# Block-sparse attention and a rational feed-forward layer on one core: GpSimd leaves the decoding of weights and the splitting of keys and queries to the vector and the activation engine

## Chip, cores, metric

One core of one Trainium2 chip. The metric is the time on the device, in microseconds, of one execution of the program; lower is better. Engines are named as in the profile: PE (matrix products), PEld (its weight loads), DVE (the vector engine), ACT (the activation engine), POOL (GpSimd), SP (the engine that issues all DMAs here).

## What is computed

Attention of 4 batches, 8 heads, 768 positions and 64 dimensions, masked by blocks of 32, then a feed-forward layer whose activation is a rational function:

```python
scores = scale * np.matmul(q, k.transpose(0, 1, 3, 2))
mask = np.abs(blk_i - blk_j) <= 1
mask = mask | (blk_i == 0) | (blk_j == 0) | (blk_i == n_blocks - 1) | (blk_j == n_blocks - 1)
# and for each block of queries three sampled blocks of keys
attn = softmax(np.where(mask, scores, -1e9))
x = np.matmul(attn, v)                      # as 3072 tokens of 512
h = x @ w_in                                # 512 x 2048
P = a[0] + a[1] * h + a[2] * h**2 + a[3] * h**3
Q = 1.0 + np.abs(b[0]) * np.abs(h) + np.abs(b[1]) * h**2
out = (P / (Q + 1e-06)) @ w_out             # 2048 x 512
```

`w_in` and `w_out` come as 64-bit numbers, so the kernel decodes them to 32 bits itself.

## The kernel before

**Weights.** `weights()` loads 32 pieces of 128 x 512 numbers (16 of `w_in`, 16 of `w_out`) as pairs of 32-bit words into two buffers `wl`. `convert` (one input) makes a 32-bit float of the upper word; `pack1`, `pack2`, `pack3` (L447, L450, L453, all DVE) put the lost bits in. A piece of `w_out` lies in `dw` then, and is split into a high part `wo_h` (`out_high`, one input) and a low part `wo_l = dw - wo_h` (`out_low`, L464, two inputs). A piece of `w_in` is decoded in place in `wi`; when four are there, ACT has taken their largest value and DVE has made a scale of it (`scw`), `three` scales each (`scaled`, `dw<-wi,scw`), takes a 16-bit high part (`high`, `wi<-dw`) and subtracts it (`low`, L511, two inputs).

**Keys and queries.** They are scaled and split in the same way into 16-bit high and low parts, 128 x 512 a tile: keys in `rest()` (tile `hl`), queries in `prep_q()` (tile `hlq` out of `ldq`, of which there is one buffer). The high part is a one-input instruction, the low part (L391) is DVE's. PE then transposes them.

**Attention and units.** `attention()` works on one block of 32 queries of all heads: scores (`sp`, L913), their maxima on DVE (L923), exponentials on ACT (`pr`, L941), transposes (`pt`, `pT`), products with values (`av`, L1039). ACT copies sampled key blocks for batch 0 (`kx`, L866). The feed-forward runs in 96 units of 256 tokens by 256 columns: PE's products into `ph` (L1150 to L1152), ACT's `sq`, `tt`, `ab`, `rr`, seven DVE instructions, the last of which are L1185 (`gh`), L1188, L1191 and L1195 (`gl`), and PE's products with `wo_h` and `wo_l` (L1206 to L1208).

**What sets the order.** Nothing is scheduled by hand: each piece of work is an `Op` with an engine, a price in nanoseconds, what it comes after, buffers it takes and a priority. `issue()` goes through them like a simulation and writes the program in the order in which they come up, each engine's queue in order. An `Op` whose engine is a dictionary may go to any engine in it; the first one is preferred. `among` makes that dictionary, but only for keys that stand in `ALT = "copsk"`; for any other key it gives the home engine alone:

```python
ALT = "copsk"

def among(key, home, **prices):
    d = {{"ve": VE, "sc": SC, "po": PO}[n]: p for n, p in prices.items()}
    return {home: d[home], **(d if key in ALT else {})}
```

`times` is the helper that does all one-input work, so its instructions have its lines: L150 on ACT, L154 on POOL and DVE (L152 for a plain copy). While POOL works, `issue` delays a DVE piece that reads no PSUM by half of what is left of POOL's (`HELD`). PE gets products that nothing uses (`fill`, L162) where it would wait early on. Because all prices enter one plan, a changed price or engine moves rows on all engines.

Of the kernel before, what the change touches and what calls it, by code (L numbers as in the profile page):

```python
# [23 lines left out]
def kernel(  # L24
# [389 lines left out]
    def weights():  # L414
# [12 lines left out]
        def one(prio, kind, u, x, before):  # L427
            d = {}
            s_wl = Slot(r_wl)
            s_w = Slot(r_dw) if kind else None  # L430

            def load():
                d["ld"] = early.tile([P, 2 * WC], I32, name="wl", bufs=2)
                if kind:
                    nc.sync.dma_start(out=d["ld"], in_=wo64[x * P:(x + 1) * P])
                    return
                for g in range(2):
                    nc.sync.dma_start(out=d["ld"][g * D:(g + 1) * D], in_=wi64[(g * HG + x) * D:(g * HG + x + 1) * D, u * 2 * WC:(u + 1) * 2 * WC])

            def convert(eng):  # L440
                d["w"] = early.tile([P, WC], I32, name="dw", bufs=3) if kind else wi[:, x, u].rearrange("p a n -> p (a n)").bitcast(I32)
                d["words"] = d["ld"].rearrange("p (n w) -> p n w", w=2)
                times(eng, d["w"].bitcast(F32), d["words"][:, :, 1].bitcast(F32), 2.0 ** -112)

            def pack1():
                w = d["w"]
                nc.vector.tensor_scalar(out=w, in0=w, scalar1=3, scalar2=None, op0=ALU.logical_shift_left)  # L447

            def pack2():
                nc.vector.scalar_tensor_tensor(out=d["w"], in0=d["words"][:, :, 0], scalar=29, in1=d["w"], op0=ALU.logical_shift_right, op1=ALU.bitwise_or)  # L450

            def pack3():
                nc.vector.scalar_tensor_tensor(out=d["w"], in0=d["words"][:, :, 1], scalar=-2 ** 31, in1=d["w"], op0=ALU.bitwise_and, op1=ALU.bitwise_or)  # L453

            def most():
                if u not in sums:
                    sums[u] = early.tile([P, 8], F32, name="sums")
                bound(d["w"].bitcast(F32), sums[u][:, x:x + 1])

            def out_high(eng):  # L460
                times(eng, wo_h[:, x], d["w"].bitcast(F32), 1.0)

            def out_low(eng):
                eng.tensor_tensor(out=wo_l[:, x], in0=d["w"].bitcast(F32), in1=wo_h[:, x].bitcast(F32), op=ALU.subtract)  # L464

            o0 = Op(SY, [(475, 524288)] if kind else [(475, 262144)] * 2, load, (), prio - 2, takes=[s_wl], behind=before)
            w = [s_w] if kind else []
            o = Op(among("c", SC, sc=520, po=588, ve=335), 0, convert, [o0], prio, takes=w, uses=[s_wl])
            o = Op(VE, 335, pack1, [o], prio, uses=w)
            o = Op(VE, 602, pack2, [o], prio, uses=[s_wl] + w)  # L470
            o = Op(VE, 602, pack3, [o], prio, uses=[s_wl] + w)
            if kind:
                o1 = Op(among("o", SC, sc=520, po=588, ve=335), 0, out_high, [o], prio, uses=w)
                o2 = Op(among("p", PO, po=1225, ve=602), 0, out_low, [o1], prio, uses=w)
                out_ready[x] = [o2]
                decoded.append(o2)
                return o0, o2
            return o0, Op(SC, 613, most, [o], prio)
# [9 lines left out]
    def w_scaled(u, prio, group, sums):  # L488
# [10 lines left out]
        for x in range(NCC):  # L499
            def three(x):  # L500
                d, s_ws = {}, Slot(r_dw)

                def scaled(eng):
                    d["w"] = early.tile([P, WC], I32, name="dw", bufs=3).bitcast(F32)
                    times(eng, d["w"], wi[:, x, u].rearrange("p a n -> p (a n)").bitcast(F32), sc[0])

                def high(eng):
                    times(eng, wi[:, x, u, 0], d["w"], 1.0)

                def low(eng):  # L510
                    eng.tensor_tensor(out=wi[:, x, u, 1], in0=d["w"], in1=wi[:, x, u, 0], op=ALU.subtract)  # L511

                a = Op(among("s", PO, po=671, ve=396, sc=613), 0, scaled, [o], prio, takes=[s_ws])
                a = Op(among("h", SC, sc=520, po=588, ve=335), 0, high, [a], prio, uses=[s_ws])
                a = Op(among("l", PO, po=1113, ve=602), 0, low, [a], prio, uses=[s_ws])
                in_ready.setdefault(u, []).append(a)
                decoded.append(a)
            three(x)
# [119 lines left out]
    def rest(b, w, j, d, o_scale, sc, prio, before):  # L638
# [20 lines left out]
        def low():  # L659
            split16(d["ld"], sc[0], d["hl"], w, None)  # L660

        o = Op(among("k", SC, po=671, ve=396, sc=613) if w == 0 else among("K", PO, po=914, ve=600), 0, high, [o_scale, o_ld], prio, takes=[s_hl], uses=[s_ld])
        o = Op(VE, 663 if w == 0 else 800, low, [o], prio, uses=[s_ld, s_hl])
        if w == 1:
            def store():
# [47 lines left out]
    def prep_q(b, t, prio, before):  # L713
# [59 lines left out]
            o, sc = scales(lambda: d["mx"][:, 0:1], "scq", [o], prio, sl_sc)  # L773
        else:
            o, sc = q_scale[b]
        h = Op(among("q", PO, po=671, ve=396, sc=613), 0, high, [o, o_ld], prio, takes=[s_hl], uses=[s_ld] + sl_sc)
        l = Op(VE, 663, low, [h], prio, uses=[s_ld, s_hl] + sl_sc)
        if own or t == 0:
            d["oc"] = row(VE, [(70, factor), (69, factor2), (69, factor3)], [o, k_scale[b]], prio, takes=d["cslot"], uses=sl_sc)
# [597 lines left out]
```

## Time and profile before

| what | value |
|---|---|
| time, median of 3 runs | 876.48 us (875.83 to 877.59) |
| time of the profiled execution | 878.83 us |
| its span, first to last instruction | 877.0 us |
| mean granted clock of PE | 0.976 |
| PE busy | 825.4 us (94%) |
| PEld busy | 644.6 us (73%) |
| DVE busy | 729.0 us (83%), 1731 instructions |
| ACT busy | 675.4 us (77%), 1447 instructions |
| POOL busy | 111.4 us (13%), 118 instructions |
| DMA | 151.16 MB, mean 172 GB/s |

The span differs from the time of the execution by what lies around the first and the last instruction. A busy share is the union of an engine's instructions, including time in which an instruction is held up after it has begun.

### The profile page before, as it was taken

The numbers are of one execution on the slowest core, as the hardware profiler recorded it, in microseconds if no ns is written. First come the engines' busy times: TensorE is split into PE (matmuls) and PEld (weight loads), VectorE is DVE, ScalarE is ACT, GpSimd is POOL, SyncE is SP. The second block draws the span as 40 slices with busy tenths as digits, with TensorE's granted clock in tenths as the row PEclk, the third lists the DMA queues.
The fourth block names the chain that finished last, engine by engine and source line by source line (L and its number), as shares of the span: only waits on it lengthen the run. The fifth ranks groups of instructions, "written<-read, shape, count | busy, mean of one in ns | idle before, by whom it ended". The sixth has DMA issues, their size and how long they took to land.

```text
span 877.0 us, 27047 instructions
## 1 busy us (share of the span) xinstructions
PE 825.4 (94%) x10334; PEld 644.6 (73%) x10334; DVE 729.0 (83%) x1731; ACT 675.4 (77%) x1447; POOL 111.4 (13%) x118
## 2 busy tenths in 40 slices
PE   8988687588899999999999999999999999999997
PEld 3545566366687888888788887878778888788886
DVE  5758987999998888888887877887878887778886
ACT  6777977797787897798777788998768687767563
POOL 1124622635220000000000000000000000000000
PEclk9999898699999999999999999999999999999999
DMA  7888689586765965889755976899555965630000
GB/s 201 209 158 209 194 177 199 127 238 196 203 156 152 273 203 157 210 214 241 200 146 139 241 204 190 198 248 248 152 131 162 224 170 160 183 102 26 1 25 25
DMA packets 240209, 151.16 MB, mean 172 GB/s; under 512 B 16208, under 2 KB 222928, under 8 KB 240080
## 3 DMA queue, kind: packets, MB, share of 16 engines
q1 hardware_dynamic: 240080, 149.43, 66.4%
q8 instruction: 82, 1.34, 0.7%
q14 instruction: 47, 0.39, 0.2%
HBM read 132.07 MB, written 11.01 MB: 163 GB/s over the span
## 4 chain that ended last, share of the span: by engine, by line
PE 69%; DVE 9%; DMA 9%; ACT 5%; SPq 4%; issue 3%; POOL 1%; ACTq 0%; DVEq 0%; POOLq 0%
PE acc L1206 9%; PE ph L1150 9%; PE acc L1208 8%; PE acc L1207 8%; PE ph L1152 8%; PE ph L1151 8%; PE av L1039 5%; PE pt L982 5%; PE sp L913 5%; DMA vg<-in_v_dram 2%; DMA wl<-in_moe_w_in_dram 2%; ACT pr L941 1%; DVE pr L923 1%; SPq L1009 1%; PE sp L758 1%
## 5 line engine op out<-in xcount | busy, mean ns | idle before, releaser
L1150 PE MATMUL ph<-xh,wi 128*128 128x256 f16 x768 | 212.1, 276 | 3.7 <-DVE tt L1167 3.6
L1152 PE MATMUL ph<-xh,wi 128*128 128x256 f16 x768 | 210.9, 275 | 0.5 <-POOL wi L511 0.5
L1151 PE MATMUL ph<-xl,wi 128*128 128x256 f16 x768 | 210.9, 275 | 0.0
L1206 PE MATMUL acc<-wo_h,gh 128*128 128x512 f32 x376 | 161.2, 429 | 1.4 <-ACT wo_h L150 1.4
L1208 PE MATMUL acc<-wo_h,gl 128*128 128x512 f32 x376 | 151.2, 402 | 2.6 <-DVE gl L1195 2.6
L1207 PE MATMUL acc<-wo_l,gh 128*128 128x512 f32 x376 | 150.5, 400 | 1.5 <-POOL wo_l L464 1.5
L1174 DVE SCALAR_TENSOR_TENSOR ab<-sq,absb,ab 128x512 f32<-128x512 f32 x96 | 73.0, 760 | 51.4 <-ACT ab L1171 51.2
L1157 ACT ACTIVATE sq<-ph,fc 128x512 f32<-128x512 f32 x96 | 65.7, 684 | 63.8 <-PE ph L1152 63.3
L1150 PEld LDWEIGHTS <-wi 128*128 128x128 f16 x768 | 75.7, 99 | 28.8 <-issue 16.3
L923 DVE CUSTOM_DVE_ANT_1 pr<-sp,bias 128x256 f32<-128x256 f32 x224 | 84.6, 418 | 13.3 <-PE sp L913 11.5
L941 ACT ACTIVATE pr<-pr,st,cqb 128x256 f32<-128x256 f32 x112 | 66.1, 593 | 29.1 <-DVE st L952 29.0
L1208 PEld LDWEIGHTS acc<-wo_h,gl 128*128 128x128 f32 x376 | 71.9, 191 | 20.3 <-DVE gl L1195 3.0
L1206 PEld LDWEIGHTS acc<-wo_h,gh 128*128 128x128 f32 x376 | 72.2, 192 | 17.8 <-ACT wo_h L150 1.6
L1185 DVE SCALAR_TENSOR_TENSOR gh<-tt,par,rr 128x512 fp32r<-128x512 f32 x96 | 73.2, 763 | 13.9 <-PE acc L1207 11.2
L982 PE MATMUL pt<-ident,pr 128*128 128x128 f32 x448 | 76.5, 292 | 8.6 <-ACT pr L941 6.9
L1151 PEld LDWEIGHTS <-wi 128*128 128x128 f16 x768 | 75.7, 99 | 11.7 <-issue 3.8
L1039 PE MATMUL av<-vg,pT 128*32 128x64 f32 x3584 | 74.1, 224 | 10.2 <-DMA vg<-in_v_dram 6.2
L1152 PEld LDWEIGHTS <-wi 128*128 128x128 f16 x768 | 75.7, 99 | 10.3 <-POOL wi L511 1.0
L982 PEld LDWEIGHTS pt<-ident,pr 128*128 128x128 f32 x448 | 67.7, 205 | 20.2 <-ACT pr L941 10.1
L1207 PEld LDWEIGHTS acc<-wo_l,gh 128*128 128x128 f32 x376 | 72.3, 192 | 13.8 <-POOL wo_l L464 1.8
L1039 PEld LDWEIGHTS av<-vg,pT 128*32 128x32 f32 x3584 | 56.3, 111 | 35.2 <-issue 15.3
L150 ACT ACTIVATE pT<-pt 128x512 f32<-128x512 f32 x112 | 66.3, 592 | 15.3 <-PE pt L982 13.6
(167 smaller groups left out, 1663.3 us busy)
## 6 DMA issues: line engine op xcount, KB each, us to landing
vg<-in_v_dram SPq DMA_DIRECT2D x312, 64.0 KB, 3.3
vg<-in_v_dram SPq DMA_DIRECT2D x88, 192.0 KB, 3.7
vg<-in_v_dram SPq DMA_DIRECT2D x24, 512.0 KB, 5.5
kall<-ks SPq DMA_DIRECT2D x52, 192.0 KB, 3.3
kall<-ks SPq DMA_DIRECT2D x156, 64.0 KB, 2.2
ld<-in_k_dram SPq DMA_DIRECT2D x36, 256.0 KB, 4.5
wl<-in_moe_w_in_dram SPq DMA_DIRECT2D x32, 256.0 KB, 4.5
wl<-in_moe_w_out_dram SPq DMA_DIRECT2D x16, 512.0 KB, 5.0
```

The source lines that it names most:

```text
L923: nc.vector.tensor_tensor_reduce(out=prs[x][:, g].rearrange("p (s r) -> p s r", r=BLK), in0=h["sp"][:, g].rearrange("p (s r) -> p s r", r= ...
L941: nc.scalar.activation(out=prs[x][:, g], in_=prs[x][:, g], func=AF.Exp, scale=Q["first"]["c"], bias=st[:, 6 + g:7 + g], accum_out=total if ...
L982: nc.tensor.transpose(pp[:, jj * P:(jj + 1) * P], cols, ident)
L1039: nc.tensor.matmul(av[rows, g], pT[:, 2 * g + kt, rows] if plain else pT[:, 2 * g + kt, pa_, rows], vf[:, g * HG + h4, kt * D:(kt + 1) * D ...
L1150: nc.tensor.matmul(o, wh, xh[:, :, cc], start=(cc == 0), stop=False)
L1151: nc.tensor.matmul(o, wh, xl[:, :, cc], start=False, stop=False)
L1152: nc.tensor.matmul(o, wl, xh[:, :, cc], start=False, stop=(cc == NCC - 1))
L1174: nc.vector.scalar_tensor_tensor(out=d["ab"], in0=d["sq"], scalar=absb[:, 1:2], in1=d["ab"], op0=ALU.mult, op1=ALU.add)
L1185: nc.vector.scalar_tensor_tensor(out=d["gh"], in0=d["tt"], scalar=par[:, 0:1], in1=d["rr"], op0=ALU.add, op1=ALU.mult)
L1206: nc.tensor.matmul(acc[:, t], ghs, wo_h[:, f], start=(new and e == 0), stop=False)
L1207: nc.tensor.matmul(acc[:, t], ghs, wo_l[:, f], start=False, stop=False)
L1208: nc.tensor.matmul(acc[:, t], gls, wo_h[:, f], start=False, stop=(last and e == 1))
```

## The change

POOL is taken out of every choice of engines but one that isn't used here ("K"). The subtractions `out_low` and `low` go to DVE alone. The scaling of `w_in` pieces and the high parts of keys go to ACT, with DVE as the other choice; the high parts of queries go to ACT alone. Converts and `out_high` stay with ACT, with DVE as the other choice.

```diff
-            o = Op(among("c", SC, sc=520, po=588, ve=335), 0, convert, [o0], prio, takes=w, uses=[s_wl])
+            o = Op(among("c", SC, sc=520, ve=335), 0, convert, [o0], prio, takes=w, uses=[s_wl])
...
-                o1 = Op(among("o", SC, sc=520, po=588, ve=335), 0, out_high, [o], prio, uses=w)
-                o2 = Op(among("p", PO, po=1225, ve=602), 0, out_low, [o1], prio, uses=w)
+                o1 = Op(among("o", SC, sc=520, ve=335), 0, out_high, [o], prio, uses=w)
+                o2 = Op(among("P", VE, ve=602), 0, out_low, [o1], prio, uses=w)
...
-                a = Op(among("s", PO, po=671, ve=396, sc=613), 0, scaled, [o], prio, takes=[s_ws])
-                a = Op(among("h", SC, sc=520, po=588, ve=335), 0, high, [a], prio, uses=[s_ws])
-                a = Op(among("l", PO, po=1113, ve=602), 0, low, [a], prio, uses=[s_ws])
+                a = Op(among("s", SC, ve=396, sc=613), 0, scaled, [o], prio, takes=[s_ws])
+                a = Op(among("h", SC, sc=520, ve=335), 0, high, [a], prio, uses=[s_ws])
+                a = Op(among("L", VE, ve=602), 0, low, [a], prio, uses=[s_ws])
...
-        o = Op(among("k", SC, po=671, ve=396, sc=613) if w == 0 else among("K", PO, po=914, ve=600), 0, high, [o_scale, o_ld], prio, takes=[s_hl], uses=[s_ld])
+        o = Op(among("k", SC, ve=396, sc=613) if w == 0 else among("K", PO, po=914, ve=600), 0, high, [o_scale, o_ld], prio, takes=[s_hl], uses=[s_ld])
...
-        h = Op(among("q", PO, po=671, ve=396, sc=613), 0, high, [o, o_ld], prio, takes=[s_hl], uses=[s_ld] + sl_sc)
+        h = Op(among("q", SC, ve=396, sc=613), 0, high, [o, o_ld], prio, takes=[s_hl], uses=[s_ld] + sl_sc)
```

Counted over the whole program, POOL loses 109 instructions; DVE gains 32 subtractions, 4 converts in `wi`, 2 in `dw`, 3 scalings and 3 key splits; ACT gains 65; PE gains 5 fills. Two places of the new order follow.

The first is ACT's queue where the first four pieces of `w_in` have got their scale, about a dozen instructions behind the `kx` copies. Before, it stood so (the scalings and the query's high part were POOL's):

```order
L397 ACTIVATE scrap,sums<-wi 128x512
L150 ACTIVATE wi<-dw 128x512 x2
L397 ACTIVATE scrap,mx<-ld 128x512
L150 ACTIVATE xh_115<-sp,xscale 128x512
L150 ACTIVATE wi<-dw 128x512
L397 ACTIVATE scrap,mx<-ld 128x512 x2
L397 ACTIVATE scrap,sums<-wi 128x512
L150 ACTIVATE wi<-dw 128x512
L762 ACTIVATE qa<-sp 128x2x512
```

In the changed program the same place reads:

```order
L150 ACTIVATE dw<-wi,scw 128x512 x2
L150 ACTIVATE wi<-dw 128x512 x2
L150 ACTIVATE xh_115<-sp,xscale 128x512
L150 ACTIVATE wi<-dw 128x512
L150 ACTIVATE dw<-wi,scw 128x512
L397 ACTIVATE scrap,sums<-wi 128x512
L150 ACTIVATE wi<-dw 128x512
L150 ACTIVATE hlq<-ldq,scq 128x8x64
L397 ACTIVATE scrap,mx<-ld 128x512
L150 ACTIVATE wi<-wl 128x512
L397 ACTIVATE scrap,mx<-ld 128x512 x2
```

Three scalings, a query's high part and a convert have come into ACT's queue ahead of the sums over `ld`.

The second is DVE's queue where the last four pieces of `w_in` have got their scale. Before:

```order
L494 COPY wscale<-scw 128x1 x2
L1185 SCALAR_TENSOR_TENSOR gh<-tt,par,rr 128x512
L453 SCALAR_TENSOR_TENSOR dw<-wl,dw 128x512
L1188 SCALAR_TENSOR_TENSOR ab<-ab,gh 128x512
L923 ISA pr,st<-sp,bias 128x256
```

In the changed program:

```order
L494 COPY wscale<-scw 128x1 x2
L1123 SCALAR_TENSOR_TENSOR fc<-wscale,sc_450,coef 128x4x2
L154 TENSOR_SCALAR dw<-wi,scw 128x512 x2
L511 TENSOR_TENSOR wi<-dw,wi 128x512 x3
L1185 SCALAR_TENSOR_TENSOR gh<-tt,par,rr 128x512
L1188 SCALAR_TENSOR_TENSOR ab<-ab,gh 128x512
L511 TENSOR_TENSOR wi<-dw,wi 128x512
L1191 SCALAR_TENSOR_TENSOR tt<-tt,par,ab 128x512
```

Two scalings and the four subtractions have come into DVE's queue, three of them ahead of the unit's `gh`.

## Rows read from the trace of the kernel before

**Rows 1.** From the page, the span in 40 slices of 21.9 us: PE's busy share in tenths, and the granted clock in tenths.

```profile
PE   8988687588899999999999999999999999999997
PEclk9999898699999999999999999999999999999999
```

**Rows 2.** Busy time by stretch. Columns: the stretch and its length; busy us and number of instructions of PE, PEld, DVE, ACT and POOL; granted clock; DMA share; GB/s.

```profile
0.00:33.00 33.00, 29.25 (x230) 14.34 (x230) 19.87 (x80) 21.99 (x50) 6.05 (x15) 1.00 0.73 192
33.00:100.00 67.00, 55.34 (x952) 34.06 (x951) 50.01 (x143) 53.83 (x144) 26.62 (x27) 0.97 0.84 194
100.00:153.40 53.40, 42.27 (x676) 33.79 (x677) 44.11 (x119) 42.16 (x103) 13.99 (x15) 0.84 0.88 191
153.40:241.20 87.80, 68.37 (x847) 53.23 (x849) 87.31 (x190) 72.77 (x156) 40.63 (x36) 0.88 0.71 191
241.20:263.10 21.90, 21.66 (x261) 17.57 (x258) 21.90 (x50) 18.15 (x39) 4.38 (x4) 1.00 0.66 156
263.10:877.00 613.90, 608.49 (x7381) 491.63 (x7379) 505.82 (x1154) 466.45 (x960) 19.75 (x23) 1.00 0.63 165
```

**Rows 3.** The chain of work that ended last, from 33 to 153.4 us: first its shares by line, then pieces in order of time (start, length, what).

```profile
by line: DMA wl<-in_moe_w_in_dram 16.9%; issue 9.8%; ACT pr L941 6.7%; DMA wl<-in_moe_w_out_dram 6.2%; DMA vg<-in_v_dram 5.1%; ACT kx L866 4.2%; DMA qc<-qa 4.0%; DMA ldq<-in_q_dram 4.0%; DVE pr L923 3.2%; POOL dw L154 3.2%; POOL wi L511 2.8
...
61.71 2.03 POOL dw L154 x3
63.74 2.24 POOL wi L511 x2
65.98 0.98 issue
67.00 1.14 POOL wi L511
68.14 1.11 POOL dw L154
69.25 1.11 POOL hlq L154
70.38 1.15 DVE hlq L391
```

**Rows 4.** Instructions in order of time between 155 and 171 us: start, length, engine, line, what.

```profile
155.56 2.71 POOL L511 TENSOR_TENSOR wi<-dw,wi 128x512 f16<-128x512 f32 x2 [0.73 <-ACT wi L150]
155.57 1.69 DVE L453 SCALAR_TENSOR_TENSOR dw<-wl,dw 128x512 int32<-128x512 int32 x1
...
168.55 0.41 DVE L447 TENSOR_SCALAR wi<-wi 128x512 int32<-128x512 int32 x1
169.49 0.68 DVE L450 SCALAR_TENSOR_TENSOR wi<-wl,wi 128x512 int32<-128x512 int32 x1
170.09 0.74 DVE L391 SCALAR_TENSOR_TENSOR hl<-ld,sc,hl 128x512 f16<-128x512 f32 x1
170.76 0.68 DVE L453 SCALAR_TENSOR_TENSOR wi<-wl,wi 128x512 int32<-128x512 int32 x1
```

**Rows 5.** DVE's groups of instructions from 153.4 to 241.2 us. Columns: line, engine, operation, tiles, shapes, count | busy us, mean ns of one | idle time before them.

```profile
L453 DVE SCALAR_TENSOR_TENSOR dw<-wl,dw 128x512 int32<-128x512 int32 x9 | 9.0, 1005 | 0.0
L450 DVE SCALAR_TENSOR_TENSOR dw<-wl,dw 128x512 int32<-128x512 int32 x9 | 7.2, 798 | 0.0
L1185 DVE SCALAR_TENSOR_TENSOR gh<-tt,par,rr 128x512 fp32r<-128x512 f32 x7 | 6.8, 965 | 0.0
L1191 DVE SCALAR_TENSOR_TENSOR tt<-tt,par,ab 128x512 f32<-128x512 f32 x7 | 6.7, 953 | 0.0
L1188 DVE SCALAR_TENSOR_TENSOR ab<-ab,gh 128x512 f32<-128x512 f32 x7 | 6.2, 882 | 0.0
L391 DVE SCALAR_TENSOR_TENSOR hl<-ld,sc,hl 128x512 f16<-128x512 f32 x6 | 5.7, 943 | 0.0
L1195 DVE TENSOR_TENSOR gl<-tt,rr 128x512 fp32r<-128x512 f32 x7 | 5.2, 748 | 0.0
L952 DVE TENSOR_SCALAR st<-st,cq 128x2 f32<-128x2 f32 x7 | 4.1, 581 | 0.0
```

**Rows 6.** The same from 264 us to the end.

```profile
L1191 DVE SCALAR_TENSOR_TENSOR tt<-tt,par,ab 128x512 f32<-128x512 f32 x82 | 61.9, 755 | 0.8
L1185 DVE SCALAR_TENSOR_TENSOR gh<-tt,par,rr 128x512 fp32r<-128x512 f32 x81 | 60.5, 747 | 13.1 <-PE acc L1207 11.2 <-ACT kt L150 0.9 <-ACT rr L1181 0.4
L1195 DVE TENSOR_TENSOR gl<-tt,rr 128x512 fp32r<-128x512 f32 x82 | 56.4, 688 | 2.2
L1188 DVE SCALAR_TENSOR_TENSOR ab<-ab,gh 128x512 f32<-128x512 f32 x81 | 55.5, 685 | 0.3
L391 DVE SCALAR_TENSOR_TENSOR hl<-ld,sc,hl 128x512 f16<-128x512 f32 x12 | 8.8, 742 | 2.3 <-POOL hl L154 1.8 <-ACT hl L150 0.4
L952 DVE TENSOR_SCALAR st<-st,cq 128x2 f32<-128x2 f32 x19 | 4.7, 245 | 0.0
```

**Rows 7.** POOL's subtractions from 153.4 to 263.1 us, in the same columns.

```profile
L464 POOL TENSOR_TENSOR wo_l<-dw,wo_h 128x512 fp32r<-128x512 f32 x10 | 14.8, 1479 | 16.8 <-ACT wo_h L150 16.5
L511 POOL TENSOR_TENSOR wi<-dw,wi 128x512 f16<-128x512 f32 x8 | 11.0, 1394 | 1.4 <-ACT wi L150 1.4
```

**Rows 8.** ACT's groups of the same kinds over the whole span.

```profile
L397 ACT ACTIVATE scrap<-ldq 128x512 f16<-128x512 f32 x12 | 7.5, 628 | 1.7 <-DMA ldq<-in_q_dram 1.7
L150 ACT ACTIVATE wi<-dw 128x512 f16<-128x512 f32 x16 | 9.8, 626 | 1.5 <-POOL dw L154 1.4
L150 ACT ACTIVATE hl<-ld,sc 128x512 f16<-128x512 f32 x8 | 5.7, 716 | 0.7 <-ACT scrap L397 0.7
```

## What was predicted

> **What bounds the kernel now.** I read the slices of the page first. From the twelfth slice on, about 241 us, PE is at 9 in every slice but the last; before it, at 5 to 9, with a granted clock between 0.6 and full [rows 1]. The table by stretch says it in numbers: from 263.1 us to the end PE is busy 608.49 of 613.9 us; before it, it loses time in every stretch, some as idle time and some as a lower clock, 0.84 from 100 to 153.4 us and 0.88 from 153.4 to 241.2 us, which are means of its two levels, 1.2 and 2.4 GHz [rows 2]. So the time is what the first 263 us take, plus a PE-bound rest that both kernels share: in both orders, where the vector engine has written its sixteenth `gl`, all weights are decoded and the same attention blocks have had their maxima, and the work left is the same but for some key and query splits.
>
> Second, who holds the first stage up. In the chain of work that ended last, the loads `wl` and the activation engine's `pr` and `kx` lead from 33 to 153 us, and once, from 61.71 to 70.36 us, GpSimd alone: four scalings, three subtractions and a query split, 7.6 us [rows 3]. From 153.4 to 241.2 us it is the vector engine: busy 87.31 of 87.80 us, beside 40.63 us of GpSimd [rows 2].
>
> Third, why it is so full. `dw` L453 begins at 155.57, beside a GpSimd subtraction that began at 155.56 (two of them run 2.71 us), and takes 1.69 us; at 170.76 the same instruction, beside no GpSimd row, takes 0.68 [rows 4]. The engine counts as busy, but for half of such an instruction it waits for GpSimd.
>
> **What the change takes away.** Of GpSimd's 118 instructions only 9 of set-up stay; 32 subtractions and 77 one-input instructions go. In the changed order the 32 and 12 of the others are on the vector engine, 65 on the activation engine.
>
> *Vector engine, 153.4 to 241.2 us, what is given back.* Means of this stretch [rows 5] less undisturbed ones, which are 0.68 for L453 and L450 [rows 4] and the groups behind 264 us for the others [rows 6]: L453 on `dw` 9 x (1005-680) = 2.9 us; L450 on `dw` 9 x (798-680) = 1.1; L1185 7 x (965-747) = 1.5; L1191 7 x (953-755) = 1.4; L1188 7 x (882-685) = 1.4; L391 6 x (943-742) = 1.2; L952 7 x (581-245) = 2.4. Together 11.9 us; L1195, 7 x (748-688) = 0.4, shows that lines I leave out add a little. I take 12 to 14.
>
> *What is put on.* GpSimd has 18 subtractions in this stretch and the 22 us behind it [rows 7]; in the changed order 15 to 17 fall to the same units. The nearest row is the two-input L1195 undisturbed, 688 ns [rows 6]; in a run without pauses the next instruction begins 0.60 us after such a one (169.49 to 170.09) [rows 4]. So 15 x 0.60 = 9 to 17 x 0.69 = 11.7 us; I take 10. Two scalings come with them (second place of the order): between 0.41, the one-input shift L447 at 168.55 [rows 4], and the 0.69 of a subtraction; I take 0.41, since they read one tensor too: 0.8 us. Net: 12 to 14 off, 9.8 to 13.1 on, so between +1 and -4 us. I take **-2.5 us**.
>
> The page "Perfetto Trace Analysis" of the Trainium skill (Optimizing Scalar/DVE Operations) speaks against the change: where VectorE is saturated, work may be given to Scalar or even to GpSimd, and here a saturated engine gets work back. By that sentence alone the sum would be 11 us on, 887 us. It goes on that the two share an SBUF read port, so that moving work between them might not help; the 1.69 and 0.68 us above agree with that half.
>
> *The chain from 33 to 153 us.* The 7.6 us of GpSimd become work of two engines. In the new order (first place) the activation engine does two scalings, two high parts, one `xh`, a high part, a scaling, a sum, a high part and then the query split. Such instructions last 0.63 to 0.72 us [rows 8]; by the 0.60 us between starts that the vector engine shows [rows 4], taken for this engine as an estimate, nine of them are 5.4 us and the split ends 0.7 later: 6.1 instead of 7.6. The low part behind it, 1.15 us on the chain [rows 3], falls to 0.74, L391 undisturbed [rows 6]. **-2 us**; 0 if the activation engine is behind with other work there, which the next term prices.
>
> *What the activation engine pays.* Up to 153.4 us GpSimd has 57 instructions [rows 2]; less 9 of set-up and the 14 subtractions that rows 7 leaves of 32, 34 have one input. Of the vector engine's 12, 8 stand there; 26 go to the activation engine, x 0.6 = 16 us. It is busy 117.98 of 153.4 us now [rows 2]; it would be 134, or 87%. Its queue is in order: behind a convert that waits for its load stand exponentials, `kx` copies and evacuations, for which PE and the vector engine wait. The lower end is 0, if each fits an idle gap, the upper end all 16. In the chain of that stretch its two largest entries hold 6.7 + 4.2 = 10.9% [rows 3], and 10.9% of 16 is 1.7. I take **+2 us**, near the low end, because loads lead that chain. From 153.4 to 263.1 us it is busy 90.9 of 109.7 us [rows 2]; 22 one-input instructions of GpSimd (40 less 18) less the 2 scalings, x 0.6 = 12 us, make 103: nearly full, still under the vector engine.
>
> *Behind 263 us.* 23 splits, 19.75 us of GpSimd [rows 2], go to the activation engine, two of them to the vector engine: at 0.72 us [rows 8] 15 us on 466 busy of 613.9. PE's 608.49 busy us hide them; without that cover each costs its 0.7 us. A split that reaches the head of the queue before its query has landed holds the engine up, but the sums over `ldq`, which wait for the same load today, had 1.7 us of idle before 12 of them [rows 8]. Nothing.
>
> **Sum:** -2.5 - 2 + 2 + 0 = -2.5 us. The profiled execution took 878.83 us (span 877.0); I apply the difference to the median of the runs, 876.48: **874.0 us**.
>
> **Rivals.**
>
> *The activation engine becomes the bound before 153 us (27%).* For it: 87% busy on average, already 53.83 of 67 us from 33 to 100 [rows 2], and a chain that runs through its queue. Against it: some of its own waits were for GpSimd, and loads lead. If 10 of its 16 us fall on the chain: -2.5 - 2 + 10 = +5.5, **882**. It decides from 4.5 us on.
>
> *Nothing to be measured (20%).* 17 subtractions at 0.69 and two scalings, 12.5 us, against 12 given back, and 2 lost for the 2 won: +0.5, **877**. Under 0.2% (1.75 us) either way can't be told from no change in this kernel.
>
> *The vector engine's long instructions stay long (4%).* Then GpSimd is not what stretches them, and the saturated stretch gets 10.8 us longer: **887**. Against it: the same lines where GpSimd is idle [rows 4, 6].
>
> **How the numbers follow.** Faster by more than 0.2% has 49%; its own range is 870.5 (vector engine -4, chain -2, activation engine 0) to 874.7. The tie has 20%, slower 31% with both rivals. The 8 in 10 leave out the last rival and the far end of the first; below I leave 2.5 us for the small stretched lines that are not in the sum: 868 to 883.
>
> **What would show it.** Right: L453, L1185, L1188 and L1191 have the same mean before and after 263 us (680 to 760 ns); the subtractions L464 and L511 take some 0.69 us; the vector engine's total stays near today's although it has 44 more instructions; the activation engine has some 35 to 45 us more; fewer slices with a low granted clock, and PE at 9 before 241 us. Wrong: the activation engine at 9 in the slices before 153 us while PE or the vector engine waits for `pr`, `kx` or `pT`; loads `wl` that start later because a convert stood in a queue; idle slices of PE behind 263 us.

## The result: slower by half a percent

The changed kernel takes 881.87 us (median of 5 runs, 880.73 to 883.16), the kernel before 877.59 beside it (875.83 to 878.71): ratio 1.0052, 95% interval 1.0033 to 1.0072. Predicted were 874.0. The sign is wrong: it went the way of the first rival, and close to that rival's 882 us. The profiled execution of the changed kernel took 880.76 us with a span of 878.8. That is 1.9 us more than the profiled one before (878.83), where the medians differ by 4.3 us: what the two profiles are read for below covers less than half of the loss.

From its page, engine totals and the slices of PE, ACT and the granted clock:

```profile
PE 825.7 (94%) x10339; PEld 643.4 (73%) x10339; DVE 720.6 (82%) x1775; ACT 709.5 (81%) x1512; POOL 2.0 (0%) x9
...
PE   8988868778989999999999999999999999999997
...
ACT  6879999998788888898877987898777688767563
...
PEclk9999977979999999999999999999999999999999
```

DVE has 44 more instructions and 8 us less busy time; ACT has 34 us more. ACT stands at 9 in the six slices from 66 to 198 us. PE is at 9 already in the eleventh slice, but falls to 8 again in the twelfth, where it was at 9 before [rows 1]. There are as many slices of low clock as before. The table by stretch of the changed kernel, in the columns of [rows 2]:

```profile
0.00:33.00 33.00, 28.55 (x224) 13.86 (x224) 18.32 (x76) 23.68 (x55) 1.97 (x9) 1.00 0.71 192
33.00:100.00 67.00, 58.08 (x900) 35.16 (x884) 51.12 (x161) 60.39 (x153) 0.00 (x0) 0.95 0.83 184
100.00:153.40 53.40, 41.47 (x658) 32.49 (x658) 45.33 (x126) 49.06 (x113) 0.00 (x0) 0.81 0.99 215
153.40:241.20 87.80, 70.91 (x958) 54.86 (x950) 81.57 (x210) 79.18 (x174) 0.00 (x0) 0.92 0.74 192
241.20:263.10 21.90, 17.72 (x271) 13.81 (x271) 19.49 (x46) 19.37 (x41) 0.00 (x0) 1.00 0.67 172
263.10:877.00 613.90, 608.95 (x7366) 493.22 (x7364) 504.73 (x1162) 477.84 (x980) 0.00 (x0) 1.00 0.62 163
```

Against [rows 2], DVE from 153.4 to 241.2 us is down from 87.31 to 81.57 us with 20 instructions more, PE there is up from 68.37 to 70.91 at a higher clock. From 33 to 153.4 us ACT is up from 95.99 to 109.45 us. And from 241.2 to 263.1 us PE, full before, has lost 3.9 us.

Three of the DVE groups of [rows 5] and the two subtractions, now (153.4 to 241.2 us, same columns):

```profile
L453 DVE SCALAR_TENSOR_TENSOR dw<-wl,dw 128x512 int32<-128x512 int32 x9 | 6.2, 685 | 0.0
L464 DVE TENSOR_TENSOR wo_l<-dw,wo_h 128x512 fp32r<-128x512 f32 x9 | 6.2, 684 | 0.0
L1185 DVE SCALAR_TENSOR_TENSOR gh<-tt,par,rr 128x512 fp32r<-128x512 f32 x8 | 6.0, 746 | 0.3 <-ACT rr L1181 0.3
L511 DVE TENSOR_TENSOR wi<-dw,wi 128x512 f16<-128x512 f32 x8 | 5.2, 688 | 0.5 <-ACT wi L150 0.3
L952 DVE TENSOR_SCALAR st<-st,cq 128x2 f32<-128x2 f32 x8 | 1.8, 222 | 0.0
```

1005 ns have become 685, 965 have become 746, 581 have become 222, and a subtraction takes the 0.69 us that was assumed. So what was to be taken off DVE did come off. Who leads instead is told by the chain of work that ended last from 153 to 218 us, by line (cut off by the view itself at its end), first before, then now:

```profile
by line: issue 9.5%; DVE dw L453 9.3%; DVE pr L923 8.5%; DVE gh L1185 7.5%; DVE tt L1191 7.0%; DVE dw L450 6.2%; DVE hl L391 5.7%; DVE ab L1188 4.7%; DVE wi L450 3.9%; DVE gl L1195 3.7%; DVE st L952 3.2%; DVE tt L1167 3.2%; DVE wi L453 3.0%
```

```profile
by line: ACT pr L941 12.1%; ACT scrap L397 11.4%; ACT dw L150 9.4%; DMA ldq<-in_q_dram 9.1%; ACT wi L150 8.2%; issue 6.2%; ACT kt L150 5.0%; ACT kx L866 5.0%; ACT ab L1171 4.9%; ACT tt L1161 4.6%; ACT rr L1181 4.0%; ACT rr L1178 3.9%; ACT s
```

Every engine's line that the view shows was DVE's and is now ACT's; `dw L150` and `wi L150`, over a sixth together, are work on weights, the scalings that POOL had among it. From 33 to 153 us, where the loads `wl` led before [rows 3], the same view has now:

```profile
by line: ACT pr L941 10.6%; DMA vg<-in_v_dram 8.4%; issue 5.4%; DMA ld<-in_k_dram 5.3%; DMA ldq<-in_q_dram 4.6%; ACT kx L866 4.4%; PE av L1039 3.9%; PE acc L162 3.5%; SPq L1009 3.1%; ACT qa L762 3.0%; DVE wi L511 2.7%; ACT pT L150 2.5%; ACT
```

**Where PE loses its time.** The two orders differ, so a comparison needs something that is the same in both. The table below counts, from the trace, the products that PE has begun by a time t (fills left out), prices each line with the mean time from the start of such a product to the start of the next one, taken behind 400 us in the kernel before, and subtracts the sum from t: the time that PE has lost by then. Changed minus before in the last column.

```
lost by t (us)   before   changed   difference
 33               26.4      26.4       0.0
153               74.2      77.8      +3.6
241              100.9      97.8      -3.1
264              101.2     102.5      +1.3
end              103.6     105.4      +1.8
```

The chain up to 153 us costs 3.6 us, the stretch of the long DVE instructions gives 6.7, the 23 us behind it take 4.4 back, and behind 264 us 0.5 is lost. One profile carries an error of some microseconds here: the kernel of the fifteenth run below, the same up to some 265 us, has 78.3, 99.3 and 104.2 at the three middle places, that of the fourteenth, the same up to some 285 us, 75.4, 96.1 and 101.2, and the order of the kernel before, run once more up to there (seventeenth), 73.1, 97.7 and 98.0. So the loss of 4 to 5 us from 241 to 264 us stands; the loss up to 153 us lies between 1 and 5, and the gain between them is 4 to 7. For PE's waits from 241.2 to 263.1 us the changed kernel has these rows (what, how long in all, how often, longest), the kernel before only `av` on `pT` with 0.2:

```profile
PE av L1039 <- ACT pT L150: 1.9, 1, 1.9
PE pt L982 <- ACT pr L941: 1.2, 1, 1.2
PE acc L1208 <- DVE gl L1195: 0.7, 1, 0.7
```

### The profile page after: what moved, and what is told of

Its sections match the earlier page's. It is cut to its first block, busy times and chain, and to the rows that moved or that the text cites. A ratio compares the mean times of both kernels' runs of the same rounds, so it can differ in the third digit from the quotient of the medians.

```text
span 878.8 us, 26989 instructions
## 1 busy us (share of the span) xinstructions
PE 825.7 (94%) x10339; PEld 643.4 (73%) x10339; DVE 720.6 (82%) x1775; ACT 709.5 (81%) x1512; POOL 2.0 (0%) x9
## 4 chain that ended last, share of the span: by engine, by line
PE 64%; ACT 17%; DMA 6%; SPq 5%; DVE 5%; issue 3%; ACTq 0%
PE ph L1150 8%; PE acc L1206 8%; PE acc L1207 8%; PE acc L1208 8%; PE ph L1151 7%; PE ph L1152 7%; PE av L1039 5%; PE pt L982 4%; PE sp L913 4%; ACT pr L941 3%; DMA ldq<-in_q_dram 2%; ACT scrap L397 2%; DMA vg<-in_v_dram 1%; ACT dw L150 1%; ACT kx L866 1%
## 5 line engine op out<-in xcount | busy, mean ns | idle before, releaser
L1185 DVE SCALAR_TENSOR_TENSOR gh<-tt,par,rr 128x512 fp32r<-128x512 f32 x96 | 71.7, 747 | 17.6 <-PE acc L1207 12.4
L1161 ACT ACTIVATE tt<-ph,par,fc 128x512 f32<-128x512 f32 x96 | 75.2, 784 | 0.0
```

The source lines that it names most:

```text
L1161: nc.scalar.activation(out=d["tt"], in_=d["ph"], func=AF.Identity, scale=d["cst"][:, 3:4], bias=par[:, 2:3])
```

## The experiments

All ratios are to the kernel before, run beside it on the same chip. Where runs of different chips are set against each other, the difference of their ratios times 877.6 us is meant.

### One part of the change alone, and no new order

**Subtractions alone** (the kernel before, with `p` and `l` on DVE):

```diff
-                o2 = Op(among("p", PO, po=1225, ve=602), 0, out_low, [o1], prio, uses=w)
+                o2 = Op(among("P", VE, ve=602), 0, out_low, [o1], prio, uses=w)
...
-                a = Op(among("l", PO, po=1113, ve=602), 0, low, [a], prio, uses=[s_ws])
+                a = Op(among("L", VE, ve=602), 0, low, [a], prio, uses=[s_ws])
```

> Only the 32 subtractions go from GpSimd to the vector engine; scalings, converts and high parts may stay on GpSimd as before. The plan is made anew. Theory A (the activation engine's added 65 instructions cost the time): the activation engine's busy time stays within 5 us of 675, the vector engine's falls below 729 because half of GpSimd's work no longer stands beside it, and the time is at or below that of the kernel before, 870 to 878 us. Theory O (any new plan around the same work costs some 4 us, whatever engine gets it): 880 to 884 us.

879.6 us, ratio 1.0011 (0.9986 to 1.0035): no change that can be told. DVE 721.7 us busy, 7 less, although it has 31 instructions more.

**One-input work alone** (the changed kernel, with these two lines back on POOL):

> Only the one-input work goes to the activation engine (with the vector engine as the other choice, as in the changed kernel); the 32 subtractions stay with GpSimd. Theory A: the activation engine is as full as in the changed kernel (some 705 us) and the vector engine still waits beside 45 us of GpSimd subtractions, so this is the slowest: 882 to 888 us. Theory O: some 4 us over before, 880 to 884. If the subtractions on the vector engine were what costs the time: 874 to 878.

885.78 us, ratio 1.0080 (1.0056 to 1.0104). In these two plans the loss comes with the one-input instructions. That the subtractions on DVE give some 2.5 us of it back is not shown: the interval overlaps the changed kernel's, and each of the two runs has a plan of its own. Where the loss falls differs too: ACT is nearly as full up to 153 us as in the changed kernel (129.7 us against 133.1, before 118.0), yet PE has lost 74.8 us by then, no more than before the change (73.1 and 74.2); it loses 34.6 us from there to 264, against 24.9 and 27.0.

**The old order.** The kernel before, planned as before, with only the engine exchanged when an instruction is written:

```diff
-            o.run(unit_of[e]) if o.alt else o.run()
+            o.run((nc.vector if o.run.__name__ in ("low", "out_low") else nc.scalar) if e == PO else unit_of[e]) if o.alt else o.run()
```

> The plan of the kernel before, unchanged; only what it gives to GpSimd is written at the same place to the vector engine (subtractions) and the activation engine (all the rest, 76 instructions). The rows of PE and of the DMA queue are the same as before. Theory A: the work on the activation engine costs the time in the old order too, 880 to 886 us, and the activation engine leads the chain from 153 to 218 us. Theory O: with the old order the time falls to the 873 to 876 us that the sum of instruction lengths gives.

889.41 us, ratio 1.0121 (1.0088 to 1.0155). The bare exchange costs 10.6 us, and the planner's new order takes 6 of them back. Theory O falls. PE's waits for ACT from 33 to 153.4 us, and below them its waits for the loads `vg`, first here:

```profile
PE av L1039 <- ACT pT L150: 5.8, 3, 3.4
PE pt L982 <- ACT pr L941: 4.4, 3, 2.6
PE sp L913 <- ACT kx L866: 3.6, 4, 1.6
PE pt L982 <- ACT pT L150: 3.2, 3, 1.7
PE av L1039 <- DMA vg<-in_v_dram: 2.6, 4, 1.2
```

and in the kernel before:

```profile
PE pt L982 <- ACT pr L941: 4.5, 3, 2.8
PE av L1039 <- ACT pT L150: 3.7, 3, 1.3
PE sp L913 <- ACT kx L866: 1.7, 2, 1.0
PE pt L982 <- ACT pT L150: 0.9, 2, 0.7
...
PE av L1039 <- DMA vg<-in_v_dram: 6.0, 3, 3.5
```

17.0 us against 10.8 for ACT, with the same rows on PE in the same order: the products wait for `pr`, `pT` and `kx`, as the prediction's last paragraph said they would if it was wrong. Part of that is other waiting that ACT now covers, as the `vg` rows show: by the count of products PE loses 3 us more than the kernel before from 33 to 153 us, and 2 before 33 us.

**Scalings and queries' high parts on DVE** (the changed kernel, planned anew):

```diff
-                a = Op(among("s", SC, ve=396, sc=613), 0, scaled, [o], prio, takes=[s_ws])
+                a = Op(among("S", VE, ve=396), 0, scaled, [o], prio, takes=[s_ws])
...
-        h = Op(among("q", SC, ve=396, sc=613), 0, high, [o, o_ld], prio, takes=[s_hl], uses=[s_ld] + sl_sc)
+        h = Op(among("Q", VE, ve=396), 0, high, [o, o_ld], prio, takes=[s_hl], uses=[s_ld] + sl_sc)
```

> The changed kernel, but the 16 scalings of w_in pieces and the 24 high parts of queries go to the vector engine instead of the activation engine (37 instructions move). On the vector engine such an instruction took 0.48 us in the changed kernel, on the activation engine 0.73. Theory A: the activation engine loses some 24 us, 10 to 13 of them before 263 us; the vector engine gains 16; the time falls to 873 to 879 us. Theory O: 880 to 884 us. If the vector engine is as tight as the activation engine: above 882.

878.08 us, ratio 1.0001 (0.9980 to 1.0023): the loss is gone. Taken alone this speaks for ACT as the only bound; the runs below take part of that back.

### What a microsecond more costs

**Thirteen scalings moved, order kept** (the changed kernel; `scaled` is written to DVE wherever the plan has it):

> The changed kernel with its own order on every engine, except that the scalings that the plan gave to the activation engine are issued to the vector engine, each at its place of the old order. The activation engine loses 13 x 0.73 = 9.5 us before 264 us, the vector engine gets 13 x 0.45 = 5.9 us. Theory A (the activation engine's queue is what costs the time): 877 to 880 us, and the chain from 153 to 218 us holds clearly less than the 53 us of that engine. Rival (the time goes to the order, or to the subtractions in the vector engine's queue): 882 us or more, since the order stays and the vector engine gets fuller.

885.63 us, ratio 1.0078 (1.0059 to 1.0098): some 2 us slower than the changed kernel, with intervals that overlap, instead of 2 to 5 faster. In its profile 2.3 us are lost before 33 us, ahead of the first row that differs (at 61 us), so what stands is that nothing was gained. Theory A falls in its plain form. From 60 to 140 us ACT's high parts wait for scalings that now stand in DVE's queue (`ACT wi L150 <- DVE dw L154`, 5.6 us in all), and the chain from 60 to 100 us runs through DVE and two loads.

**Idle subtractions on POOL** beside each of DVE's 32:

```diff
+    scrap = const.tile([P, 512], F16, name="scrap"); spy = early.tile([P, 256], F16, name="spy", bufs=1); beside = lambda low: [nc.gpsimd.tensor_tensor(out=spy, in0=low[:, n:n + 256], in1=low[:, n:n + 256], op=ALU.subtract) for n in (0, 256)]
...
+                    eng.tensor_tensor(out=wi[:, x, u, 1], in0=d["w"], in1=wi[:, x, u, 0], op=ALU.subtract); beside(wi[:, x, u, 1])
```

(the same behind `wo_l`).

> The changed kernel plus, behind each of the 32 subtractions, two 128x256 subtractions on GpSimd that read the finished low part and write a scratch tile that nobody reads: the two other engines keep their instructions and their order, nothing waits for GpSimd. It measures by itself what GpSimd costs by working beside the vector engine. If GpSimd stretches the vector engine (the part of the prediction that gave 12 us back from 153 to 241 us): the vector engine's busy time rises by 10 to 25 us, L453, L1185 and L1191 go back to 0.9 us and above, and the time rises to 885 to 890 us. If the long instructions of before came from something else: no change, 881 to 883 us.

894.71 us, ratio 1.0187 (1.0165 to 1.0210), 12 us more than without, by work for which nobody waits. DVE's busy time is up by 17.2 us. Two of its groups from 153.4 to 263.1 us and POOL's idle work:

```profile
L1191 DVE SCALAR_TENSOR_TENSOR tt<-tt,par,ab 128x512 f32<-128x512 f32 x8 | 7.7, 966 | 0.0
L453 DVE SCALAR_TENSOR_TENSOR dw<-wl,dw 128x512 int32<-128x512 int32 x10 | 7.6, 762 | 0.0
...
L393 POOL TENSOR_TENSOR spy<-wo_l 128x256 f16<-128x256 f32 x32 | 29.7, 928 | 81.0 <-DVE wo_l L464 53.7 <-DVE sm L1069 7.1 <-DVE sm L963 7.0
L393 POOL TENSOR_TENSOR spy<-wi 128x256 f16<-128x256 f16 x32 | 27.6, 861 | 92.9 <-DVE wi L511 90.6
```

966 ns instead of 747 for L1191; L453 with 762 instead of 685 and L1185 with 780 instead of 747 were hit less than expected, presumably because the idle work starts when a subtraction has ended and so meets what stands behind one. This is the price of company that the prediction read from [rows 4], now measured by itself. The page "SBUF — State Buffer" of the Trainium skill ("Who interferes with whom") says that DVE and GpSimd share one pair of ports, and that a DVE instruction with two inputs in SBUF contends there with a GpSimd instruction that reads SBUF; L1191 has two such inputs, and its 966 and 747 ns agree.

**High parts twice** on ACT:

```diff
-                    times(eng, wi[:, x, u, 0], d["w"], 1.0)
+                    for _ in range(2 if eng is nc.scalar else 1): times(eng, wi[:, x, u, 0], d["w"], 1.0)
```

(the same for `wo_h`).

> The changed kernel, in which the activation engine writes each high part of the weights twice (the second time the same values): up to 32 more instructions of 0.63 us there, 20 us, nearly all of them before 264 us, and nothing else changed. Theory A (that engine bounds this part): a large share of the 20 us arrives at the end, 887 to 895 us. Rival (the engine has slack and the loss is elsewhere): 882 to 884 us.

895.64 us, ratio 1.0177 (1.0155 to 1.0199): ACT has 18.2 us more, the time 11.0 more than the changed kernel, 0.6 us for each. From 153.4 to 241.2 us ACT is now the fuller engine by far (DVE 71.82, ACT 82.46):

```profile
153.40:241.20 87.80, 68.20 (x860) 52.23 (x858) 71.82 (x185) 82.46 (x180) 0.00 (x0) 0.83 0.67 174
```

With the run before it (11.8 us for 17.2 on DVE, 0.7 each) this says that in this order both engines are dear before 264 us.

**Scalings on DVE, splits free** (`among("S", VE, ve=396)` and `among("c", SC, ve=396, sc=613)` for the queries):

> The changed kernel with the scalings of the weights on the vector engine and the queries' splits free for the planner to give to either of the two engines. Theory A: before 264 us the activation engine is relieved as in the run with both on the vector engine (878 us), and the late splits stand where there is room: 873 to 878 us. Rival (only which plan comes out matters, not the engine's load): anywhere from 874 to 884 us, with no shift of the chain away from the activation engine.

889.74 us, ratio 1.0128 (1.0106 to 1.0150): neither expectation. PE is level with the kernel before at 264 us (101.6 us lost), and loses 12 behind it, 5 of them between 340 and 370 us, where ACT's sum over `ldq` waits 5.8 us for its load.

### What a microsecond less gives

Three runs of the changed kernel with every row in its place, some of them shorter. The first line leaves seven eighths of the columns out of each maximum, the second the signs of 448 of 512 columns of `w_in`:

```diff
-                bound(d["w"].bitcast(F32), sums[u][:, x:x + 1])
+                bound(d["w"].bitcast(F32)[:, :64], sums[u][:, x:x + 1])
...
-                nc.vector.scalar_tensor_tensor(out=d["w"], in0=d["words"][:, :, 1], scalar=-2 ** 31, in1=d["w"], op0=ALU.bitwise_and, op1=ALU.bitwise_or)
+                n = 512 if kind else 64; nc.vector.scalar_tensor_tensor(out=d["w"][:, :n], in0=d["words"][:, :n, 1], scalar=-2 ** 31, in1=d["w"][:, :n], op0=ALU.bitwise_and, op1=ALU.bitwise_or)
```

The first line alone:

> The changed kernel, every row in its old place; the 16 sums of the activation engine over the decoded input weights (scrap<-wi, L397, 0.63 us) read 64 of 512 columns. The rest of the maximum is left out. That takes some 16 x 0.4 = 6.5 us off the activation engine before 245 us and leaves the vector engine alone. Theory A1 (the activation engine alone bounds this part, the vector engine has slack): 4 to 5 us less than the changed kernel, 877 us. Theory A2 (both engines are full and take turns, so that a microsecond added to either costs 0.7, as the two runs with added work showed, but one taken from either alone gives back little): 879 to 882 us.

The second alone:

> The changed kernel, every row in its old place; the 16 sign steps of the vector engine on the input weights (L453 on wi, 0.69 us) treat 64 of 512 columns, the rest of the signs is left out. Some 16 x 0.42 = 7 us off the vector engine, none off the activation engine. A1: 881 to 882 us, as the vector engine has slack. A2: 878 to 881 us, some of it, and clearly less than both together.

Both:

> Both of the last two edits in one kernel: some 6.5 us off the activation engine and 7 off the vector engine, rows in their old places, the same work left out. A1: as the run with the activation engine's cut alone, 877 us. A2: more than the sum of the two single cuts, 872 to 876 us.

881.78, 882.54 and 882.09 us; ratios 1.0062 (1.0038 to 1.0086), 1.0057 (1.0036 to 1.0079) and 1.0060 (1.0038 to 1.0081): none differs from the changed kernel's 1.0052. The cuts were there, as a group of the first and one of the second run shows (16 x 0.38 us off ACT, 16 x 0.47 off DVE):

```profile
L397 ACT ACTIVATE scrap<-wi 128x64 f16<-128x64 f32 x16 | 4.1, 254 | 0.2
...
L453 DVE SCALAR_TENSOR_TENSOR wi<-wl,wi 128x64 int32<-128x64 int32 x16 | 3.5, 221 | 0.1
```

Both theories fall: A1 wanted 4 to 5 us of the first, A2 6 to 10 of the third. In all three PE has lost 77.4 to 77.6 us by 153 us, as in the changed kernel (77.8), and from 241 to 264 us it still loses 4.4 to 5.5. In the third run's chain from 100 to 264 us the loads `wl` of `w_in` are the largest entry (10.3%), which would explain why work on those pieces gives nothing back; that is an argument, not a measurement.

**Scalings and output high parts on DVE**, planned anew (`"S"` as above, `among("O", VE, ve=335)` for `out_high`):

> The changed kernel, planned anew with the 16 scalings of the input weights and the 16 high parts of the output weights on the vector engine, where such an instruction takes 0.45 us against 0.63 to 0.73 on the activation engine. Both engines together have some 6 us less to do than in the changed kernel, the activation engine some 20 us less, the vector engine 14 more. A1: 874 to 878 us, since the activation engine is relieved. A2: no better than 880 us, as the vector engine becomes the full one; a plan by itself moves the time by several us either way, so that this run can speak against A1 but not prove A2.

886.2 us, ratio 1.0113 (1.0083 to 1.0143): 14 us less on ACT than in the changed kernel (695.2 against 709.5), and slower. DVE has 83.24 of 87.8 us from 153.4 to 241.2 us. This speaks against ACT as the only bound.

### Waits at the head of ACT's queue

**The run with scalings and splits on DVE, with later query loads in the plan.** Only from 250 us of the plan's time on, the planner counts a query load as landing 4 us later, so that it puts other work ahead of the sum that waits for it:

```diff
-                        lat = MARGIN if isinstance(price, list) else OWN.get(e, 0) if y == e else LAT.get((e, y), 160) + MARGIN
+                        lat = MARGIN + (4000.0 if o.start > 250000 and o.run.__qualname__.endswith('prep_q.<locals>.load') else 0.0) if isinstance(price, list) else OWN.get(e, 0) if y == e else LAT.get((e, y), 160) + MARGIN
```

> The run with scalings and queries' splits on the vector engine, planned anew from 250 us of the plan's own time on with one thing changed: the planner counts each query load as landing 4 us later, so that it sets the activation engine's sum over ldq (L397) behind other work. Before that place all rows are the same. There, that sum held the activation engine up for 5.9 us and PE for 3. Theory H (an instruction that waits for its load at the head of the activation engine's queue is what gives the early gain back behind 264 us): no such wait above 2 us, and 3 us less than that run, 875 us. Rival (behind 264 us PE has the backlog to hide it): no difference, 878 us.

874.44 us (873.33 to 879.58, 9 runs), ratio 0.9966 (0.9940 to 0.9992): faster than both kernels, the only one of these runs that is, and than the kernel before by an interval that ends just short of 1. Without the edit, waits from 335 to 372 us read

```profile
ACT scrap L397 <- DMA ldq<-in_q_dram: 5.9, 1, 5.9
DVE scq L353 <- PE sp L348: 3.3, 1, 3.3
PEld sp L348 <- ACT scrap L397: 3.2, 1, 3.2
PE sp L348 <- ACT scrap L397: 2.9, 1, 2.9
```

and with it the longest of that stretch is

```profile
DVE ab L1174 <- ACT ab L1171: 2.2, 3, 1.3
...
ACT scrap L397 <- DMA ld<-in_v_dram: 1.0, 2, 0.6
```

The wait is gone, and the 3.3 us that PE lost from 340 to 370 us are not lost in this run, as theory H said. By the end PE has lost 98.1 us instead of 101.2; 1.8 of that stand already at 264 us, where the rows are the same, and a sum elsewhere still waits 3.4 us for its `ld`. The ratios differ by 0.35%, 3 us, with intervals that just overlap: the mechanism is seen, its size is not exact.

**The changed kernel with the same edit:**

> The changed kernel with the same edit to the planner. Theory H: where the changed kernel's PE loses some 1.5 to 3 us behind 264 us (sums that wait 3 us for a load), 880 us; if the loss sits before 264 us, no difference, 881 to 883 us.

885.96 us, ratio 1.0078 (1.0049 to 1.0108). Neither expectation, and no faster: the new plan has such waits at other loads (4.8 us for `ld` between 500 and 600 us, where PE loses 5). The edit is no remedy by itself.

**Late splits back on POOL**, order kept:

```diff
-            o.run(unit_of[e]) if o.alt else o.run()
+            o.run(nc.gpsimd if e == SC and o.run.__qualname__.endswith(('prep_q.<locals>.high', 'rest.<locals>.high')) and o.start > 250000 else unit_of[e]) if o.alt else o.run()
```

> The changed kernel with every row in its place, but the high parts of queries and keys behind some 265 us go back from the activation engine to GpSimd, as before the change. It prices the prediction's term for that part, nothing. If nothing is right: 881 to 883 us. If the splits in the activation engine's queue cost there: 878 to 880 us.

881.82 us, ratio 1.0040 (1.0019 to 1.0061): the splits behind 265 us cost nothing that can be told.

**Seven instructions ahead of 243 us back on POOL** (the same line with `out_high` and the queries' `high` between 195 and 230 us of the plan's time):

> The changed kernel with every row in its place, but six high parts of output weights and one query split, at some 205 to 243 us, go back to GpSimd. From 241 to 264 us PE of the changed kernel loses 4 us that it doesn't lose in the kernel before, and two of these seven stand directly ahead of the pr for which it waits first. Theory A (those in the activation engine's queue cost it): PE loses 2 us less there, 878 to 880 us. Rival (the vector engine's queue, full from 241 to 254 us, sets that time): 882 us or more, since GpSimd works beside it again.

880.81 us, ratio 1.0024 (1.0006 to 1.0043). Between the two expectations; its interval overlaps that of the changed kernel, and its profile still loses 5.4 us from 241 to 264 us. This settles nothing.

**Controls for the fastest run.** The kernel before with the later loads:

> The kernel before, GpSimd with all its work, with the planner's later query loads from 250 us of its own time on. It tells whether the gain of the run with scalings and splits on the vector engine and later loads is one that the kernel before could have had too. In the trace of the kernel before, no sum holds PE up behind 264 us; so theory H expects no gain: 877 to 881 us. If it comes out at 874 to 876 us, the edit to the planner alone makes the gain.

879.05 us, ratio 1.0036 (1.0015 to 1.0057): the edit doesn't help the kernel before. And the queries' splits alone on DVE, without the scalings:

> The changed kernel, planned anew with the queries' splits alone on the vector engine; the scalings stay where the change has them. With the scalings alone moved and the splits free, PE had lost as much by 264 us as before the change. If the splits, which stand ahead of exponentials in the activation engine's queue up to 100 us, cost the early time: PE is some 5 us ahead of the changed kernel at 100 us, as in the run with both moved, and the time is 876 to 880 us. If not, the gain of that run was its plan's: 881 us or more and no lead at 100 us.

881.6 us, ratio 1.0052 (1.0029 to 1.0075), and no lead at 100 us (59.8 us lost by then; 54.4 with both moved, 59.6 before). Neither the splits alone nor the scalings with the splits free (58.4, the eighth run) give that lead; with both moved the planner finds an order that has it.

## Why the prediction was wrong

*Two stages, with a rest that both kernels share: right.* The sixteenth `gl` ends at 272.3 us before and at 273.0 us now (269.3, and 274.7 and 271.7, where the same orders ran again up to there), and from there to the end the two kernels take 604.7 and 605.8 us. So the loss that the profiles show arises in the first stage, which was to get 2.5 us shorter.

*The relief of DVE: right, and too small.* Durations fell to the undisturbed ones, subtractions cost 0.69 us, the engine's total fell. Predicted were -2.5 us from 153.4 to 241.2 us; PE's lost time fell by 4 to 7 there. The rival of instructions that stay long is out. (In the row that gave the undisturbed 0.68 us, a one-input instruction of POOL did run beside the last 0.1 us; the 685 ns of now confirm the figure.)

*What ACT pays: the load right, its price wrong. This is the step that failed.* Predicted were 134 us of busy time up to 153.4 us; it is 23.68 + 60.39 + 49.06 = 133.1. But of the 16 us that came, the prediction let 10.9% cost time, the share that two of ACT's lines had in the chain of the kernel before, and took +2, "because loads lead that chain". In the changed kernel `pr` leads it with 10.6%, and the loads `wl` are no longer among the lines that the view shows. Work added to ACT's queue in the changed order costs 0.6 us per us (high parts twice), work on DVE 0.7 (idle subtractions), and 16 x 0.6 = 10 is what the first rival took. A share in the old chain tells what the engine holds up as it is; it doesn't tell what one instruction more does to an engine that is busy 90% of a stretch (60.39 of 67 us from 33 to 100) and whose queue is in order.

*The chain from 33 to 153 us: -2 and +2 predicted, +1 to +5 measured* as PE's lost time. That the eight instructions of GpSimd on the chain would be done sooner on two engines was no gain that can be seen. That ACT's own exponentials and copies stood behind them is shown in the old order, where PE waited 6 us longer for them; in the changed order it is argued from the chain, and the run with one-input work alone, with ACT nearly as full, lost nothing there. That the rival's 882 us came so close is in part luck: it had +8 us up to 153 us and nothing from 241 to 263.

*From 241 to 263 us no term at all: the second step that failed.* The prediction had ACT "nearly full, still under the vector engine" up to 263.1 us and priced nothing; ACT's busy time there is 98.6 us of 109.7, below the 103 forecast, and PE loses 4 to 5 us. The waits name `pT`, `pr` and `gl`, so both engines. Which of them causes it is **open**: less of either or of both did nothing, and seven instructions taken from ACT gave no clear answer.

*Behind 263 us: nothing predicted, 0.5 us in the profiles*, and the late splits back on POOL change nothing. Right here. But the reservation in that paragraph, that work at the head of the queue waits for its load, was worth more than was seen: in two other plans such a wait cost PE 3 to 5 us.

*The new order had no price.* The sum took the rows' places from the changed order but treated the planner as neutral. It gave 6 us back against the bare exchange; other plans of nearly the same work lie between 874 and 890 us. That spread is larger than any term of the sum, and the range (868 to 883) held the time only because it reached out to the rival. So the runs show what the exchange costs in a given order. How much of the changed kernel's 4.3 us is ACT's load, and how much the plan that happened to come out, no run separates.

*Theory A, that ACT's added instructions cost the time,* is shown for a fixed order by the old order and by high parts twice. That ACT alone bounds the kernel is refuted by the cut sums, and the moved scalings and the plan with 14 us less on ACT speak against it.

## What to carry to other kernels

Taking an engine out of play has two prices: what the other engines no longer suffer by its company (here 12 us for 57 us of idle work that imitates it), and what its work costs where it goes. The second is not that engine's share in the old chain: work added to a full, in-order queue cost 0.6 to 0.7 us per us here. The two don't make a sum: the bare exchange put 21 us more on ACT up to 263 us, which at 0.6 is about what those 57 us of company cost, and it was 10.6 us slower. Work added to such a queue can cost at once, while work taken out of a fixed order gave nothing back here, so measure the exchange in the old order and the new order apart. In an in-order queue look for the instruction that waits for a load at its head; moving other work ahead of it took a wait of 5.9 us away here, in a plan whose time then fell by some 3.

## What was not expected of the hardware

GpSimd's own instructions get longer beside DVE, too. A subtraction of 128 x 256 on POOL took 0.86 to 0.93 us in the mean, but 0.61 us at its shortest and 2.54 at its longest; the whole ones that the change removed took 1.15 (L511) and 1.27 us (L464) at their shortest and 1.39 to 1.48 in the mean [rows 7]. So at the shortest, half the size is about half the time (types differ in part), and the means hold what is added beside DVE. And 57 us of such work, for which nobody waits, cost 12 us of a kernel whose bound at the end is PE.
